# One joint tile for the q and k weights, loads in waves, more transposes by DMA and a new instruction order in an attention and MLP kernel

## Chip, core and metric

The kernel runs on one core of a Trainium2 chip. The metric is the device time of one execution in microseconds (us). Medians are quoted. Ratios are the mean time of one kernel's fast runs over that of the other's of the same rounds, with a 95% interval, so not quite the ratio of the medians. A run counts as fast within 1.5% of the fastest of its kernel.

Engines: PE is TensorE (matrix products), PEld its weight loads, DVE VectorE, ACT ScalarE, POOL GpSimd, SP SyncE, which here issues DMAs.

## The reference, cut to what matters

```python
x = A_x                                    # 2048 positions x 512, bf16
h  = x + attention(layernorm(x)) @ wo      # 32 heads of 16; 8 keys: positions s, s-2, ... s-14
h2 = h + ((relu(n @ W_gate) * (n @ W_up)) @ W_down)     # n = layernorm(h), 1376 hidden
```

## The kernel before

The 2048 positions are handled in four chunks of 512 positions (chunk 0 to 3), each of four tiles of 128 rows. Each chunk has a first norm of x, transposed so that features lie on partitions; the q, k and v products (PE); the attention, mostly large elementwise products on DVE; the output projection with the residual; a second norm of h, transposed too; and the gate, up and down products (PE).

All steps are collected in a plan, and a list of numbers, RANK, gives each step its place on its engine. So the order of every engine's queue is a part of the program, and is fixed when it runs.

Some transposes are done by DMA, issued from SP. And for chunks 0 to 2 the first additions of the attention's tree are *accumulating* DMAs, issued from POOL (`ta`), of 512 KB each:

```python
DACC = tuple((k, t) for k in range(3) for t in range(4))       # chunk, head group
TDD, TDL = 2.4, 1.6                         # planned issue and latency of a DMA transpose
DMAT = (("h",2,0),("h",2,2),("x",3,0),("x",3,2))   # h: second norm, x: first; chunk; first tile of a pair
# ... in layernorm(), for a pair of tiles in DMAT:
nc.sync.dma_start_transpose(out=dst.t[:, :, j * P:(j + 1) * P], in_=xn.t[:])
# ... else on TensorE:
nc.tensor.transpose(tp.t[:].bitcast(BF16)[:, o:o + P], xn.t[:, t * P:(t + 1) * P], identity[:])
# ... in the attention, after the value product mu{t}:
m = add(("mu%d" % t, tk), "DVE", D40, f_mu, ...)
if n == 4 and (tk, t) in DACC:
    nc.gpsimd.dma_start(mt.t[:, 0:4, :], mt.t[:, 4:8, :], accum_op=ALU.add)
```

The softmax here doesn't subtract the row's maximum and nothing guards it: scores larger than these inputs give would overflow.

Of the kernel before, what the change touches and what calls it, by code (L numbers as in the profile page):

```python
# [18 lines left out]
    1, 3, 5, 2, 0, 4, 54, 6, 7, 30, 160, 197, 186, 250, 712, 8, 11, 10, 12, 14,  # L19
    17, 23, 27, 32, 20, 26, 31, 16, 18, 21, 24, 28, 33, 37, 9, 13, 15, 19, 22, 25,  # L20
    29, 34, 35, 65, 71, 68, 70, 73, 38, 60, 66, 56, 63, 69, 51, 61, 43, 55, 40, 50,
    45, 58, 83, 145, 79, 154, 76, 162, 74, 99, 80, 86, 96, 104, 110, 75, 67, 85, 89, 90,
    171, 179, 185, 114, 136, 123, 133, 128, 94, 113, 101, 108, 118, 148, 159, 183, 189, 193, 156, 170,
    199, 203, 205, 165, 176, 201, 204, 207, 142, 152, 181, 187, 192, 211, 218, 210, 215, 214, 222, 209,
    212, 227, 234, 221, 225, 228, 232, 226, 231, 239, 241, 246, 256, 249, 257, 261, 244, 259, 251, 260,
    264, 292, 321, 277, 317, 267, 313, 324, 333, 340, 280, 305, 270, 304, 301, 308, 303, 310, 315, 295,
    325, 307, 328, 285, 323, 319, 329, 335, 327, 344, 297, 341, 331, 346, 314, 339, 349, 350, 366, 343,
    358, 338, 365, 355, 372, 392, 334, 359, 348, 362, 397, 401, 421, 691, 717, 393, 407, 694, 718, 357,
    420, 701, 721, 363, 423, 699, 720, 39, 47, 44, 48, 36, 41, 42, 46, 49, 52, 62, 78, 64,
    77, 82, 57, 81, 59, 72, 84, 144, 191, 124, 188, 91, 178, 102, 182, 88, 164, 109, 169, 143,  # L30
    172, 117, 168, 147, 252, 139, 300, 87, 299, 151, 302, 195, 174, 224, 245, 229, 208, 238, 248, 253,
    258, 268, 273, 271, 284, 293, 296, 294, 290, 275, 283, 286, 287, 289, 298, 309, 345, 352, 318, 330,
    361, 367, 326, 337, 364, 368, 306, 316, 347, 351, 373, 378, 379, 386, 376, 382, 383, 395, 385, 389,
    391, 396, 390, 394, 398, 400, 402, 403, 406, 413, 408, 415, 419, 411, 417, 412, 418, 422, 431, 456,
    427, 454, 433, 460, 426, 452, 494, 439, 469, 441, 471, 434, 462, 436, 463, 500, 438, 466, 437, 465,
    479, 488, 464, 474, 503, 487, 496, 484, 491, 489, 498, 493, 501, 507, 450, 518, 458, 517, 506, 523,
    499, 520, 526, 447, 508, 444, 509, 524, 516, 536, 709, 726, 510, 530, 707, 725, 522, 538, 705, 723,
    533, 537, 703, 722, 98, 105, 92, 97, 93, 103, 53, 95, 112, 116, 126, 132, 125, 130, 146, 131,
    137, 129, 135, 150, 167, 216, 177, 217, 184, 220, 194, 223, 161, 240, 157, 237, 163, 242, 153, 213,
    173, 428, 175, 409, 202, 416, 219, 356, 236, 254, 265, 312, 274, 263, 288, 320, 322, 332, 336, 342,  # L40
    360, 353, 377, 375, 369, 374, 371, 384, 387, 381, 380, 430, 435, 453, 459, 414, 429, 446, 449, 424,
    432, 451, 457, 399, 425, 443, 448, 467, 473, 461, 468, 475, 482, 470, 478, 477, 480, 472, 476, 485,
    486, 481, 483, 490, 495, 519, 521, 511, 513, 528, 531, 497, 502, 543, 559, 540, 558, 549, 568, 548,
    565, 573, 560, 585, 567, 582, 575, 588, 544, 561, 594, 556, 578, 583, 593, 554, 576, 579, 590, 596,
    552, 570, 563, 580, 546, 564, 553, 574, 591, 616, 625, 572, 618, 599, 621, 608, 623, 631, 620, 630,
    587, 628, 633, 626, 642, 715, 731, 612, 639, 713, 729, 597, 635, 711, 727, 600, 640, 714, 730, 100,
    106, 115, 121, 111, 119, 107, 120, 122, 127, 140, 149, 155, 166, 134, 141, 138, 158, 247, 281, 180,
    255, 196, 269, 190, 266, 243, 279, 235, 278, 200, 272, 230, 276, 233, 541, 198, 505, 262, 550, 206,
    545, 291, 282, 311, 404, 370, 354, 388, 405, 410, 440, 442, 492, 445, 504, 529, 534, 527, 532, 455,
    525, 514, 515, 512, 542, 562, 581, 586, 535, 539, 555, 569, 551, 557, 566, 571, 547, 577, 584, 589,  # L50
    595, 603, 604, 611, 598, 607, 592, 601, 606, 609, 614, 615, 610, 613, 602, 605, 617, 619, 622, 624,
    636, 637, 641, 627, 634, 629, 632, 638, 646, 660, 650, 663, 647, 661, 644, 656, 675, 667, 677, 665,
    674, 673, 681, 670, 678, 684, 659, 671, 654, 668, 657, 669, 662, 672, 682, 651, 664, 652, 666, 643,
    655, 645, 658, 679, 683, 695, 648, 686, 680, 693, 649, 689, 697, 653, 688, 676, 690, 696, 685, 706,
    728, 736, 692, 700, 716, 732, 687, 702, 719, 734, 698, 704, 724, 735, 708, 710, 733, 737,
# [36 lines left out]
class Plan:  # L92
# [21 lines left out]
    GUIDE = ()  # L114

    def order(self):
        for kx, cx, ky, cy in self.GUIDE:
            xs = [o for o in self.ops if o.key and o.key[0].startswith(kx) and o.key[1] == cx]
            for o in self.ops:
                if o.key and o.key[0].startswith(ky) and o.key[1] == cy:  # L120
                    o.deps += xs
        waiting = list(self.ops)
        free = {}
        while waiting:
            best = {}
            for op in waiting:
# [45 lines left out]
            waiting.remove(op)  # L172
# [4 lines left out]
def kernel(  # L177
# [55 lines left out]
    w3_sb = [sb.tile([P, NT, D], BF16, name=f"w{n}_sb") for n in "qkv"]  # L233
# [32 lines left out]
    def setup():  # L266
# [4 lines left out]
        for c, q in enumerate((nc.sync, nc.scalar, nc.sync)):  # L271
            q.dma_start(w3_sb[c][:], w3_r[:, :, c * D:(c + 1) * D])
        for tk in range(1, NCK):
            nc.sync.dma_start(x_sm[:, tk * BPC:(tk + 1) * BPC, :], x_rows[:, tk * BPC:(tk + 1) * BPC, :])

        nc.sync.dma_start(wo_sb[:], A_wo.rearrange("(p t) f -> p t f", t=NT))
        nc.sync.dma_start(wu_sb[:], B_W_up.rearrange("(dt p) f -> p dt f", p=P))
        nc.sync.dma_start(wg_sb[:], B_W_gate.rearrange("(dt p) f -> p dt f", p=P))
        nc.sync.dma_start(
            wd_sb[:, 0:NFF, :], B_W_down[0:NFF * P, :].rearrange("(ft p) n -> p ft n", p=P))  # L280
        if FTAIL:
            nc.sync.dma_start(wd_sb[:FTAIL, NFF, :], B_W_down[NFF * P:F, :])

# [10 lines left out]
        nc.gpsimd.memset(vT[:, :, 0:PADL], 0.0)  # L294

# [22 lines left out]
    TDD, TDL = 2.4, 1.6  # L318
    NWARM = 48
    DMAT = (("h",2,0),("h",2,2),("x",3,0),("x",3,2))  # L320
# [8 lines left out]

    LNA = ((0, 0, 0, 0), (0, 0, 0, 0))  # L330
# [5 lines left out]
    A5, A10, AX, AS = 0.52, 0.92, 0.8, 0.2  # L336
    AL = 0.14
    D2, D5, D10, D20, D40, DST, DSM = 0.34, 0.62, 0.62, 1.15, 2.2, 0.6, 0.08
    DL = 0.14

    def load(t):
        return add(None, "LD", 0.0, None, lat=t)

    xload = [[load(t) for t in (3.4, 3.5, 3.9, 3.9)]] + [[load(t)] * BPC for t in (9.7, 11.2, 12.7)]
    wload = {n: load(t) for n, t in
             (("q", 6.3), ("k", 7.0), ("v", 8.3), ("o", 14.0), ("u", 18.0), ("g", 22.0), ("d", 27.0))}

    def layernorm(tk, src, dst_slots, pr, groups, on_act, residual=None):
# [7 lines left out]
        for grp in groups:  # L356
# [3 lines left out]
            for j in grp:  # L360
# [17 lines left out]
                elif tk == 0 and j == BPC - 1:  # L378

                    xns[j], sm, sq = Buf(xn_s), Buf(sm_s), mv  # L380

                    def f_su(j=j, xn=xns[j], sm=sm):
                        nc.scalar.activation(out=xn.t[:], in_=x_sm[:, j, :], func=ACT.Copy,
                                             accum_out=sm.t[:, j:j + 1])

                    def f_nm(j=j, sm=sm):
                        V.tensor_scalar(out=mv.t[:, j, 0:1], in0=sm.t[:, j:j + 1], scalar1=1.0 / D,
                                        scalar2=None, op0=ALU.mult)

                    def f_sq(j=j, xn=xns[j]):  # L390
                        nc.scalar.activation(out=xn.t[:], in_=x_sm[:, j, :], func=ACT.Square,
                                             bias=mv.t[:, j, 0:1], scale=-1.0, accum_out=mv.t[:, j, 1:2])

                    a = add(("xsu", tk), "ACT", 0.75, f_su, [src[j]], pr, take=[xns[j], sm], lat=AL)
                    a = add(("xnm", tk), "DVE", DSM, f_nm, [a], pr, take=[mv], use=[sm], lat=DL)
                    ag.append(add(("xsq", tk), "ACT", 0.75, f_sq, [a], pr, use=[mv, xns[j]], lat=AL))
                else:
                    st = Buf(st_s)

                    def f_st(j=j, st=st):  # L400
                        V.bn_stats(out=st.t[:], in_=x_sm[:, tk * BPC + j, :])

                    def f_ag(j=j, st=st):
                        V.bn_aggr(out=mv.t[:, j, :], in_=st.t[:])

                    a = add((ln + "st" + gk, tk), "DVE", DST, f_st, [src[j]], pr, take=[st], lat=DL)
                    ag.append(add((ln + "ag" + gk, tk), "DVE", DSM, f_ag, [a], pr, take=[mv], use=[st], lat=DL))
# [433 lines left out]
```

## Time and profile before

| | before |
|---|---|
| time, first three runs | 203.86 us (203.53 to 205.39) |
| span of the profiled execution | 203.6 us |
| PE busy / DVE busy | 195.4 us (96%) / 155.1 us (76%) |
| granted TensorE clock, mean of the span | 0.983 |

PE is full from 10 us to 200 us, so the time is the moment at which PE starts, plus its work, plus the tail.

### The profile page before, as it was taken

The numbers are of one execution on the slowest core, as the hardware profiler recorded it, in microseconds if no ns is written. First come the engines' busy times: TensorE is split into PE (matmuls) and PEld (weight loads), VectorE is DVE, ScalarE is ACT, GpSimd is POOL, SyncE is SP. The second block draws the span as 40 slices with busy tenths as digits, with TensorE's granted clock in tenths as the row PEclk, the third lists the DMA queues.
The fourth block names the chain that finished last, engine by engine and source line by source line (L and its number), as shares of the span: only waits on it lengthen the run. The fifth ranks groups of instructions, "written<-read, shape, count | busy, mean of one in ns | idle before, by whom it ended". The sixth has DMA issues, their size and how long they took to land.

```text
span 203.6 us, 2957 instructions
## 1 busy us (share of the span) xinstructions
PE 195.4 (96%) x1102; PEld 96.8 (48%) x1123; DVE 155.1 (76%) x246; ACT 127.7 (63%) x253; POOL 12.6 (6%) x26
## 2 busy tenths in 40 slices
PE   8499999999999999999999999999999999999994
PEld 8347545555545334444454444444444445444452
DVE  6549999999999999999999966599996255021314
ACT  3517879986569993797756599703665353576400
POOL 3000000330000002400033000000000000000000
PEclk9859999999999999999999999999999999999999
DMA  5999901698000002980059900400011001100003
GB/s 187 350 379 403 322 19 30 123 203 163 3 0 0 0 3 52 192 168 0 3 103 180 209 31 0 90 13 0 3 41 62 0 0 53 53 0 0 0 3 103
DMA packets 14893, 18.04 MB, mean 89 GB/s; under 512 B 5056, under 2 KB 12192, under 8 KB 14880
## 3 DMA queue, kind: packets, MB, share of 16 engines
q1 hardware_dynamic: 12336, 10.78, 16.4%
q0 software_dynamic: 1728, 6.29, 16.3%
q10 hardware_dynamic: 816, 0.79, 1.1%
q8 instruction: 9, 0.15, 0.3%
q14 instruction: 4, 0.03, 0.0%
HBM read 8.42 MB, written 2.10 MB: 52 GB/s over the span
## 4 chain that ended last, share of the span: by engine, by line
PE 93%; DMA 4%; issue 1%; SPq 0%; DVE 0%
PE bank L736 38%; PE bank L511 22%; PE bank L773 19%; PE bank L698 7%; DMA wq_sb<-in_A_wqkv_dram 4%; PE bank L564 4%; PE bank L465 2%; PE bank L625 1%; PE bank L597 1%; SPq L270 0%; DVE row L784 0%
## 5 line engine op out<-in xcount | busy, mean ns | idle before, releaser
L736 PE MATMUL bank<-quad,wg_sb 128*128 128x512 bf16 (+1 forms) x171 | 42.3, 379 | 0.3
L736 PE MATMUL bank<-quad,wu_sb 128*128 128x512 bf16 (+1 forms) x173 | 42.3, 379 | 0.1
L743 ACT ACTIVATE gr<-bank 128x512 bf16<-128x512 f32 (+1 forms) x44 | 26.0, 604 | 23.7 <-PE bank L736 18.3
L773 PE MATMUL bank<-wd_sb,gT 128*128 128x512 bf16 (+3 forms) x184 | 39.7, 366 | 0.2
L558 DVE TENSOR_TENSOR big<-quad,kT 128x4096 bf16<-128x4096 bf16 x16 | 36.0, 2284 | 0.1
L646 DVE TENSOR_TENSOR big<-big,vT 128x4096 bf16<-128x4096 bf16 x16 | 35.8, 2283 | 0.3 <-ACT big L631 0.3
L740 ACT CAST up_sb<-bank 128x512 bf16<-128x512 f32 (+1 forms) x44 | 25.7, 594 | 12.3 <-PE bank L736 8.5
L756 DVE TENSOR_TENSOR gT<-gr,up_sb 128x1024 bf16<-128x1024 bf16 (+1 forms) x24 | 15.4, 643 | 20.4 <-ACT gr L743 14.1
L773 PEld LDWEIGHTS <-gT 128*128 128x128 bf16 (+1 forms) x187 | 18.0, 98 | 19.3 <-issue 0.4
L736 PEld LDWEIGHTS <-wu_sb 128*128 128x128 bf16 (+1 forms) x176 | 17.3, 100 | 20.7 <-issue 1.3
L736 PEld LDWEIGHTS <-wg_sb 128*128 128x128 bf16 (+1 forms) x176 | 17.3, 100 | 20.6 <-issue 1.1
L511 PE MATMUL bank<-quad,wq_sb 128*128 128x512 bf16 (+1 forms) x70 | 16.9, 382 | 2.5 <-DMA wq_sb<-in_A_wqkv_dram 2.1
L631 ACT CAST big<-bank 128x512 bf16<-128x512 f32 x32 | 17.2, 610 | 1.5 <-PE bank L625 1.3
L511 PE MATMUL bank<-quad,wk_sb 128*128 128x512 bf16 (+1 forms) x70 | 16.8, 373 | 0.1
L678 POOL DMA_DIRECT2D big<-big x12 | 10.7, 894 | 98.3 <-DVE big L646 95.2
L784 DVE TENSOR_TENSOR row<-x_sm,bank 128x512 bf16<-128x512 bf16 (+1 forms) x17 | 10.6, 652 | 7.8 <-PE bank L773 7.8
L649 DVE TENSOR_TENSOR big<-big 128x1024 bf16<-128x1024 bf16 (+2 forms) x24 | 16.4, 727 | 0.0
L709 DVE SCALAR_TENSOR_TENSOR x_sm<-x_sm,bank 128x512 bf16<-128x512 bf16 x16 | 10.9, 685 | 6.8 <-PE bank L698 6.7
L511 PE MATMUL bank<-quad,wv_sb 128*128 128x512 bf16 x62 | 15.4, 379 | 0.1
L698 PE MATMUL bank<-wo_sb,quad 128*128 128x512 bf16 x61 | 14.8, 379 | 0.2
L371 ACT ACTIVATE row<-x_sm,mv 128x512 bf16<-128x512 bf16 x16 | 11.5, 717 | 4.5 <-DVE mv L363 4.4
L519 ACT CAST quad<-bank 128x512 bf16<-128x512 f32 x16 | 9.6, 601 | 7.4 <-PE bank L511 7.4
(65 smaller groups left out, 161.7 us busy)
## 6 DMA issues: line engine op xcount, KB each, us to landing
big<-big POOLq DMA_DIRECT2D x12, 512.0 KB, 5.5
out_dram<-row SPq DMA_DIRECT2D x15, 128.0 KB, 1.7
x_sm<-in_A_x_dram SPq DMA_DIRECT2D x3, 512.0 KB, 11.0
wu_sb<-in_B_W_up_dram SPq DMA_DIRECT2D x1, 1376.0 KB, 10.6
wg_sb<-in_B_W_gate_dram SPq DMA_DIRECT2D x1, 1376.0 KB, 13.9
wd_sb<-in_B_W_down_dram SPq DMA_DIRECT2D x1, 1280.0 KB, 15.7
wq_sb<-in_A_wqkv_dram SPq DMA_DIRECT2D x1, 512.0 KB, 8.4
wk_sb<-in_A_wqkv_dram ACTq DMA_DIRECT2D x1, 512.0 KB, 8.6
```

The lines of the kernel that those rows point to most:

```text
L371: nc.scalar.activation(out=xn.t[:], in_=h.t[:] if h else x_sm[:, tk * BPC + j, :], func=ACT.Square, bias=mv.t[:, j, 0:1], scale=1.0, accum ...
L511: nc.tensor.matmul(mm.t[:, lo:hi], lhsT=w3_sb[c][:, dt, t:D:NT], rhs=xnT.t[:, dt, lo:hi], start=(dt == 0), stop=(dt == NT - 1))
L558: V.tensor_tensor(out=pb.t[:].rearrange("p (t w) s -> p t w s", t=2), in0=q4, in1=k4, op=ALU.mult)
L631: nc.scalar.copy(out=ab.t[:, w, :], in_=bc.t[:])
L646: V.tensor_tensor(out=mt.t[:], in0=ab.t[:], in1=v8, op=ALU.mult)
L649: V.tensor_tensor(out=mt.t[:, 0:n, :], in0=mt.t[:, 0:n, :], in1=mt.t[:, n:2 * n, :], op=ALU.add)
L698: nc.tensor.matmul(od.t[:], lhsT=OT.t[:, t, j * P:(j + 1) * P], rhs=wo_sb[:, t, :], start=(t == 0), stop=(t == NT - 1 and tk not in RPE))
L736: nc.tensor.matmul(mm.t[:fs, :], lhsT=w_sb[:, dt, ft * P: ft * P + fs], rhs=hnT.t[:, dt, :], start=(dt == 0), stop=(dt == NT - 1))
L740: nc.scalar.copy(out=ub.t[:fs, i, :], in_=um.t[:fs, :])
L743: nc.scalar.activation(out=gr.t[:fs, i, :], in_=gm.t[:fs, :], func=ACT.Relu)
L756: V.tensor_tensor(out=gt.t[:fs, 0:n, :], in0=gr.t[:fs, 0:n, :], in1=ub.t[:fs, 0:n, :], op=ALU.mult)
L773: nc.tensor.matmul(od.t[:, c0:c1], lhsT=gts[ft].t[:fs, ft % 2, j * P:(j + 1) * P], rhs=wd_sb[:fs, ft, c0:c1], start=(ft == 0), stop=(ft == ...
```

## The change

It means to start PE earlier and with a warm clock, and to take 16 transposes off it: the q and k weights go to one tile, loaded by four DMAs in pieces of 2 KB; later loads are held back by small copies on POOL until earlier ones have landed ("waves"); chunk 0's first norm is made in four groups of one tile; 8 idle products after each of the first two transpose groups keep the clock up; chunk 3's second norm is transposed by DMA. The whole order is new, made with lower planned costs for a DMA transpose. The residuals were on DVE already.

```diff
-    w3_sb = [sb.tile([P, NT, D], BF16, name=f"w{n}_sb") for n in "qkv"]
+    wqk_sb = sb.tile([P, NT, 2 * D], BF16, name="wqk_sb")
+    wv_sb = sb.tile([P, NT, D], BF16, name="wv_sb")
...
+        for dt in range(NT):
+            (nc.scalar if dt % 2 else nc.sync).dma_start(wqk_sb[:, dt:dt + 1, :], w3_r[:, dt:dt + 1, 0:2 * D])
...
+        nc.gpsimd.tensor_copy(out=x_sm[0:1, BPC, 0:1], in_=x_sm[0:1, 0, 0:1])
+        nc.sync.dma_start(x_sm[:, BPC:2 * BPC, :], x_rows[:, BPC:2 * BPC, :])
+        nc.gpsimd.tensor_copy(out=wv_sb[0:1, 0, 0:1], in_=wqk_sb[0:1, NT - 1, 0:1])
+        nc.sync.dma_start(wv_sb[:], w3_r[:, :, 2 * D:3 * D])
+        nc.gpsimd.tensor_copy(out=x_sm[0:1, 2 * BPC, 0:1], in_=x_sm[0:1, BPC, 0:1])
...
-    TDD, TDL = 2.4, 1.6
-    NWARM = 48
-    DMAT = (("h",2,0),("h",2,2),("x",3,0),("x",3,2))
+    TDD, TDL = 1.25, 1.5
+    NWARM, NFILL = 44, 8
+    DMAT = (('h',2,0),('h',2,2),('x',3,0),('x',3,2),('h',3,0),('h',3,2))
...
-        groups = [[0, 1], [2], [3]] if tk == 0 else [[0, 1, 2, 3]]
+        groups = [[0], [1], [2], [3]] if tk == 0 else [[0, 1, 2, 3]]
...  (all numbers of RANK are new, and the queues follow it strictly)
```

## The prediction

> **What bounds the kernel now.** I read the page's slices first, then the chain of waits, then the start on a finer scale.
>
> The slices (40 of 5.09 us; tenths of busy time, and the clock granted to TensorE):
>
> ```profile
> PE   8499999999999999999999999999999999999994
> DVE  6549999999999999999999966599996255021314
> PEclk9859999999999999999999999999999999999999
> ```
>
> TensorE (PE) is full from the third slice to the last; VectorE (DVE) is full only up to about 110 us. The two weak spots are the second slice, where PE is at 4 tenths, and the second and third of the clock row, 8 and 5 tenths. The chain of waits, in order of time (start us, us, what; pieces left out), with the pieces that the change touches:
>
> ```profile
> 1.66 8.42 DMA wq_sb<-in_A_wqkv_dram
> 10.08 0.05 issue
> 10.13 2.32 PE bank L511 x9
> 12.45 0.22 issue
> 12.67 7.27 PE bank L511 x38
> ...
> 166.88 0.22 PE bank L465 x4
> 167.11 1.73 PE bank L773 x8
> 168.83 0.45 PE bank L465 x8
> 169.28 0.65 PE bank L773 x3
> 169.93 0.23 PE bank L465 x4
> ...
> 194.39 6.27 PE bank L773 x39
> ```
>
> One load (8.42 us), then TensorE from 10.13 to 200.66 without a wait worth naming. So the time is start of the q and k products + TensorE work + about 3 us of tail (last addition and store). Only these terms can move: when TensorE starts, how fast its clock is then, and how many instructions stand in its queue. Finer stretches (us, PE busy, clock, DMA share, GB/s):
>
> ```profile
> 8.50:9.00 0.50, 0.00 (x0) 0.80 1.05 375
> 9.00:9.50 0.50, 0.00 (x0) 0.50 1.09 387
> ...
> 15.00:15.50 0.50, 0.50 (x3) 0.50 1.10 408
> 15.50:16.00 0.50, 0.50 (x3) 0.88 1.00 397
> ```
>
> A mean of 0.80 over 8.5 to 9.0 puts the drop to half clock at 8.8; 0.88 over 15.5 to 16.0 puts the return at 15.6. From 10.13 to 15.62 the first products therefore ran at half speed: 5.5 us for 2.75 us of work.
>
> **What the Trainium skill says.** "TensorE: Matmul & The Clock Gate", Part 1 (the HAM clock gate): the array drops to half clock after a window of about 3.4 us with too little activity and returns after a busy one, and the window runs freely, so that its phase differs from run to run. The trace agrees: 8.8 to 15.6 is 6.8 us, two such windows. Same page, Part 4 (PE-mode transpose): transposes do not count as activity as matmuls do. That fits: 16 transposes ran between 6.7 and 8.1 us and the clock fell all the same; one trace can't prove it. "DMA: Bandwidth & Descriptors", Issuing engines are not separate DMA queues: all loads run on the same 16 engines and interleave. The trace agrees: q and k, issued at 1.66 us, landed after 8.4 and 8.6 us, v after 9.6, and by my sum of the GB/s some 2.66 MB had moved by 10 us, though the first x tiles, q and k are only 1.57 MB. Same page, Why small descriptors are slow: about 3 cycles per packet beside 32 bytes per cycle. 1 KB pieces then cost 35 cycles and 2 KB ones 67, so the wider pieces save 3 cycles in 70, some 4% of 1.05 MB at 350 GB/s: 0.1 us, an estimate from that page. No run shows it yet.
>
> **The change, part by part.** The title's "residuals on DVE" and the DMA transposes of chunk 2's second norm and chunk 3's first are already in the kernel before; new among those is only chunk 3's second norm.
>
> 1. Loads in waves. At first only the x tiles of chunk 0, the joint q and k tile and the x of chunk 1 are in flight (2.1 MB at most); v waits for the last quarter of the q and k tile, chunk 2's x for chunk 1's. From the stretches of 2 us (16, 282, 336, 351 GB/s), 1.57 MB have moved by 6.9 us and 2.1 MB by 8.4 us. Taking the middle and some latency, q and k are there at 8.0 us, against 10.08.
>
> 2. But then the norm of chunk 0 is the later of the two. Before, these rows of the timeline (start, us, what) show it done at 8.7 us, with TensorE then waiting for weights until 10.13:
>
> ```profile
> 3.48 1.29 DVE L401 BATCH_NORM_STATS2 st<-x_sm 128x6 f32<-128x512 bf16 x2 [0.29 <-DMA x_sm<-in_A_x_dram]
> 7.44 1.23 ACT L479 COPY quad<-bank 128x512 bf16<-128x512 bf16 x2 [0.61 <-PE bank L465]
> 7.51 0.75 DVE L477 COPY quad<-bank 128x512 bf16<-128x512 bf16 x2
> ```
>
> The change makes four groups of one tile and moves the fourth tile's statistics from ScalarE (ACT) to DVE. Read from the new order list, DVE does four statistics (0.64 each), four aggregates (0.15), three normalisations (0.35) and a copy (0.72) before the first half of the columns is complete: 2.56 + 0.60 + 1.05 + 0.72 = 4.93 us from 3.48, so 8.4, and with some gaps for ScalarE's logarithm and exponential (0.3 and 0.2 us a pair) 8.8. So TensorE's first product goes at 8.8, not at 8.0: 1.3 us earlier than before. One transpose group (0.25 us) now falls behind that start. Gain: about 1.05 us.
>
> 3. Fills. 44 warm-up products in place of 48, and 8 after each of the first two transpose groups, about 0.45 us each, all in front of the first product where TensorE idles: no cost on the path. Their gain is the clock. In the profiled run the loss was 2.75 us. If the clock holds, all of it comes back; if it still falls at 8.8, the window that follows is now full of products and ends at 12.2, so 3.4 us at half clock, 1.7 lost, 1.05 gained. But the profiled execution took 205.38 us and the three runs 203.53, 203.86 and 205.39; as the window's phase is free, I take the median run to have lost only about 2.75 - 1.5 = 1.25 us (my guess from that spread). From this I count 0.5 to 1.2 us for the median, 0.8 in the middle, with more possible.
>
> 4. Chunk 3's second norm leaves TensorE: 0.22 + 0.45 + 0.23 = 0.90 us of the chain. In its place SyncE's queue (SP) issues four DMA transposes. The eight of the kernel before were issued in 1.2 us each and landed 2.5 us after issue. After the last output-projection product of chunk 3, the way to the normalised, transposed tile is residual 0.77, mean 0.15, square 0.91, logarithm and exponential 0.50, one normalisation 0.35, four issues 4.8 and 1.3 more until landing: 8.8 us. The new order list gives TensorE 20 gate and up products and 44 down products of chunk 2 in that time: 64 x 0.2155 = 13.8 us. So it is hidden with 5 us to spare: gain 0.90 us.
>
> 5. Everything else in the list reorders work. Before, the table of TensorE's waits has only 0.4 us after the start, so order can gain nothing there and can only lose. DVE's start on the attention products moves up too: after the last copy at about 9.8 it has chunk 1's norm (some 5 us) to do and can start near 15.2 rather than at 18.84, 3.6 us earlier, so it shouldn't become the bound of the DVE-full stretch. I deduct 0.1 us for new small waits; the retuned durations in the diff suggest that the order was searched with care.
>
> Sum for the median: 1.05 + 0.8 + 0.90 - 0.1 = 2.65, with 0.6 added for the chance that the clock holds all along where the run before lost the full 2.75: about 3.25 us, giving 203.86 - 3.25 = 200.6 us, 1.6% less.
>
> **The rivals.** (a) The weights still bind. For it: q landed 3.2 us after the moment at which 1.57 MB had moved, so bytes alone do not tell the landing. If that lag stays, q and k come at about 9.5 to 10, the start gains nothing, and with 0.9 for the transposes and some clock the result is 202.5. Against it: less is in flight behind the tile. (b) The clock stays warm in every run and was cold in most of the runs before: 1.05 + 2.75 + 0.9 = 4.7, so 199.2 and over 2%. For it: the fills and the earlier products fill the critical window; against it: transposes and waits still leave that window only about half busy (my count is about 2 us of 3.4, against 1.8 before). (c) DVE becomes the bound. It now does more at the start, and up to 110 us it has no slack; if chunk 0's attention starts only 2 us earlier while TensorE is 3.5 us ahead, TensorE waits in 20 to 67 us and 1.5 us of the gain are lost: 202. Against it is the estimate of 15.2 us above. (d) The DMA transposes arrive late because SP must first issue stores that wait for DVE; every microsecond over the 5 spare is a wait of TensorE near 170 us. I give it little.
>
> **Range and chances.** The mechanical gains of 1.05 and 0.9 are rather sure; the clock's share runs from 0 to 2.75; rivals (a) and (c) take 1 to 2. That spans 198.4 to 202.9. Faster by over 2% needs about 199.8 or less (a gain of 4 us), which is the full clock gain with no loss elsewhere: 0.37. Slower by 2% would need a broken order: 0.02.
>
> **What would show it.** Step 1: q and k land at 7.5 to 8.8 us. Step 2: TensorE's first q or k product starts at 8.6 to 9.2, released by the copy of the transposed tile (DVE), not by the DMA. Step 3: the granted clock shows no half-speed slice after 6 us, or one window only; chunk 0's 32 q and k groups take about 7 us instead of 9.65. Step 4: 80 transposes of that line on TensorE instead of 96, 12 DMA transposes, and no wait before chunk 3's first up product. Step 5: TensorE's waits after the start stay below 1 us in sum. The prediction is wrong if the start doesn't move, if new waits of over 1.5 us stand in TensorE's row between 20 and 70 us, or if the start is warm and full and the time falls below 198.4.

## More of the kernel before

The prediction shows the lines. One that it does not show turned out to matter most. It closes the view of the transposed tiles of the kernel before, and gives the least, the middle and the largest time from issue to landing of its eight DMA transposes:

```profile
DMA to landing us min/median/max: 2.4/2.5/5.4
```

The middle value is what a transpose takes alone (e2 below). The largest is over twice that. The timeline shows what ran then: the queue of SP first, then that of POOL (start us, us, engine, line, what):

```profile
33.65 5.22 SPq L454 DMA_TRANSPOSE quad<-row  x4
37.48 1.01 POOL L678 DMA_DIRECT2D big<-big  x1 [35.04 <-DVE big L646]
```

The four transposes of chunk 3 are issued from 33.65 to 38.87 us, and the first accumulating DMA starts at 37.48, when the last transpose is still to come. Only the tail of the row overlaps.

## The result

212.69 us (211.59 to 214.1, six runs) against 203.85 us: the ratio is 1.043 (1.038 to 1.048). It is slower by 4.3%, far outside the range.

The slices of the profile after, in 40 parts of 5.31 us: busy tenths of PE, granted clock, and DMA engines.

```profile
PE   7699899980699999999999999999999999999993
PEclk9999999998599999999999999999999999999999
DMA  5689951998200000397000992032010022200012
```

The start is as forecast: no dip of the clock in the first slices. But the tenth slice of PE is empty: near 50 us it does nothing, while the DMA engines are busy for 8 tenths, and in the eleventh the clock is at 5 tenths. The waits of PE, over the whole span (engine, line waited for: us in total, times, longest us):

```profile
PE bank L525 <- DMA quad<-row: 8.3, 1, 8.3
PE bank L525 <- DMA wqk_sb<-in_A_wqkv_dram: 1.2, 2, 0.8
```

The chain of waits has the same place in order of time:

```profile
44.01 11.03 DMA quad<-row
55.04 0.14 issue
55.17 8.84 PE bank L525 x32
```

`quad<-row` is a DMA transpose; L525 are the q, k and v products. PE waited 8.3 us for one transposed tile of chunk 3's first norm, a step that the change left on the DMA where it was. And 32 products took 8.84 us where at full clock they take 32 x 0.216 = 6.9 (the prediction's chain has 1.73 us for 8). Finer stretches show why (us, PE busy, clock, DMA share, GB/s; a packet counts whole where it starts, so a share can pass 1):

```profile
46.00:50.00 4.00, 0.88 (x5) 1.00 1.62 72
50.00:54.00 4.00, 0.00 (x0) 0.74 0.68 98
54.00:58.00 4.00, 2.83 (x7) 0.50 0.11 22
```

After five idle microseconds the clock fell to half (0.74 of four microseconds puts it at 51.9 us), and the products after the wait began cold. It came back at about 58.8 us (0.90 over 58 to 62 us). These 6.9 us fit two of the windows of about 3.4 us of the Trainium skill ("TensorE: Matmul & The Clock Gate", Part 1). Wait and cold products together: 8.3 + 1.9 = 10.2 us, more than the whole loss.

The timeline tells when the transposes were issued, with the accumulating DMAs beside them:

```profile
36.42 0.73 DVE L455 TENSOR_SCALAR row<-x_sm,mv,rs 128x512 bf16<-128x512 bf16 x2
37.18 10.01 SPq L473 DMA_TRANSPOSE quad<-row  x4
41.47 0.73 DVE L455 TENSOR_SCALAR row<-x_sm,mv,rs 128x512 bf16<-128x512 bf16 x2
```

```profile
34.61 1.01 POOL L692 DMA_DIRECT2D big<-big  x1 [23.42 <-DVE big L660]
36.82 0.86 POOL L692 DMA_DIRECT2D big<-big  x1 [1.20 <-DVE big L660]
39.90 0.86 POOL L692 DMA_DIRECT2D big<-big  x1 [2.21 <-DVE big L660]
41.85 0.86 POOL L692 DMA_DIRECT2D big<-big  x1 [1.09 <-DVE big L660]
```

```profile
DMA to landing us min/median/max: 2.4/2.5/12.7
```

The new order puts two of chunk 3's normalisations (L455) behind two value products (L660), and the other two behind all four. So the transposes run from 37 us on, in the middle of the four accumulating DMAs, and one of them took 12.7 us to land. The accumulating DMAs of that stretch landed after 8.1 us in the middle, against 6.2 before.

### The profile page after: what moved, and what is told of

Read it like the earlier page. It is cut to its first block, busy times and chain, and to the rows that moved or that the text cites. A ratio compares the mean times of both kernels' runs of the same rounds, so it can differ in the third digit from the quotient of the medians.

```text
span 212.3 us, 2963 instructions
## 1 busy us (share of the span) xinstructions
PE 196.1 (92%) x1119; PEld 95.9 (45%) x1119; DVE 155.4 (73%) x247; ACT 121.9 (57%) x249; POOL 12.9 (6%) x29
## 4 chain that ended last, share of the span: by engine, by line
PE 61%; DVE 23%; DMA 12%; issue 2%; ACT 0%; POOL 0%; DVEq 0%; ACTq 0%; POOLq 0%
PE bank L750 27%; PE bank L787 18%; DVE big L572 10%; DVE big L660 7%; DMA x_sm<-in_A_x_dram 7%; PE bank L712 7%; PE bank L525 6%; DMA quad<-row 5%; DVE st L420 2%; DVE row L455 1%; PE bank L578 1%; DVE gT L770 1%; DVE ex L626 1%; PE bank L484 0%; PE bank L639 0%
## 5 line engine op out<-in xcount | busy, mean ns | idle before, releaser
L754 ACT CAST up_sb<-bank 128x512 bf16<-128x512 f32 (+1 forms) x44 | 24.8, 595 | 26.4 <-PE bank L750 18.8
L525 PE MATMUL bank<-quad,wqk_sb 128*128 128x512 bf16 (+1 forms) x144 | 30.9, 364 | 9.5 <-DMA quad<-row 8.3
L660 DVE TENSOR_TENSOR big<-big,vT 128x4096 bf16<-128x4096 bf16 x16 | 36.0, 2283 | 0.1
L525 PEld LDWEIGHTS <-wqk_sb 128*128 128x128 bf16 x144 | 15.8, 115 | 22.3 <-issue 10.9
L663 DVE TENSOR_TENSOR big<-big 128x1024 bf16<-128x1024 bf16 (+2 forms) x24 | 16.9, 730 | 3.5 <-DMA big<-big 3.4
L533 ACT CAST kT<-bank 128x512 bf16<-128x512 f32 x16 | 9.3, 615 | 12.5 <-PE bank L525 12.5
L525 PE MATMUL bank<-quad,wv_sb 128*128 128x512 bf16 x64 | 16.2, 396 | 0.0
L455 DVE TENSOR_SCALAR row<-x_sm,mv,rs 128x512 bf16<-128x512 bf16 x32 | 11.5, 403 | 4.2 <-ACT rs L437 4.2
```

The source lines that it names most:

```text
L455: V.tensor_scalar(out=xn.t[:], in0=x, scalar1=mv.t[:, j, 0:1], scalar2=rs.t[:, j:j + 1], op0=ALU.add if residual else ALU.subtract, op1=AL ...
L525: nc.tensor.matmul(mm.t[:, lo:hi], lhsT=wv_sb[:, dt, t:D:NT] if c == 2 else wqk_sb[:, dt, c * D + t:(c + 1) * D:NT], rhs=xnT.t[:, dt, lo:h ...
L660: V.tensor_tensor(out=mt.t[:], in0=ab.t[:], in1=v8, op=ALU.mult)
L663: V.tensor_tensor(out=mt.t[:, 0:n, :], in0=mt.t[:, 0:n, :], in1=mt.t[:, n:2 * n, :], op=ALU.add)
L754: nc.scalar.copy(out=ub.t[:fs, i, :], in_=um.t[:fs, :])
```

## The experiments

Three theories were set against each other. C, collision: transposing and accumulating DMAs in flight together hold each other up. L, late: the transposes are quick but issued too late. S, start: the new start delays everything after it.

### e1: chunk 3's normalisations ahead of the value products

```diff
 DVE, from 31 us (step/chunk; xxn = normalise for the first norm, mu = value product)
-xxn3/2 mu3/0 mu0/0 xxn0/3 xxn2/3 mu1/0 mu2/0 xxn3/3 xxn1/3
+xxn3/2 xxn0/3 xxn2/3 xxn3/3 xxn1/3 mu3/0 mu0/0 mu1/0 mu2/0
 ACT: chunk 3's logarithm and exponential right after the eighth copy of chunk 0's weights
```

> The changed kernel with one edit of its order list: the four normalisations of chunk 3's first norm go before chunk 0's first value product on DVE, and their logarithm and exponential on ScalarE right after the eighth copy of chunk 0's weights, so that the four DMA transposes are issued at about 33 to 38 us, before the accumulating DMAs, as in the kernel before. Theory C (collision: DMA transposes and the accumulating DMAs of chunk 0, in flight together, hold each other up): transposes land after about 2.5 us, the wait of 8.3 us and the half clock after it (32 products in 8.84 us instead of 6.9) go, 212.7 - 10.2 = 202.5 us (201 to 204.5). Theory L (late: the transposes are quick, only issued too late): the same 202.5. Theory S (start: the new loads and groups of the start delay everything after them): 210 or more.

Measured: 203.49 us against 203.96; ratio 0.998 (0.996 to 1.000). In the queue of SP the transposes stand early again:

```profile
33.02 5.27 SPq L473 DMA_TRANSPOSE quad<-row  x4
```

The longest landing is 5.0 us (5.4 in the kernel before), and PE no longer waits for a transpose. One move in an order list is worth 9.2 us. S is out as the cause of the loss; C and L are not yet told apart. And the forecast gain is still missing: 0.5 us instead of 3.25.

### e2: no accumulating DMAs in chunk 0

```diff
-    DACC = tuple((k, t) for k in range(3) for t in range(4))
+    DACC = tuple((k, t) for k in range(1, 3) for t in range(4))
```

> The changed kernel with chunk 0's four accumulating DMAs taken out; DVE makes these additions itself (4 x 1.15 us), at the place where the tree of additions goes on. Chunk 3's transposes are still issued late, from 37 to 42 us and on. Theory C: with nothing to collide with they land in about 2.5 us each, TensorE's wait for them falls from 8.3 to under 2 us; time 203 to 206. Theory L: the wait stays near 8 us, 211 to 214. Theory S: 211 to 214.

Measured: 209.31 us; ratio 1.026 (1.024 to 1.029). The transposes start as late as in the changed kernel, at 36.5 us, yet the view of the tile says of all twelve:

```profile
DMA to landing us min/median/max: 2.4/2.5/2.5
```

PE had no wait for them at all: its row is full from 46 to 54 us. So the lateness alone cost nothing there, and the whole wait of 8.3 us came from the accumulating DMAs, as C says. The time missed the expected 203 to 206, because the 4.6 us of additions now on DVE gave PE a wait of 3.6 us for the attention's result, and a cold stretch after it. The mechanism was right, the total was not.

### e3: chunk 3's first norm transposed by PE

```diff
-    DMAT = (('h',2,0),('h',2,2),('x',3,0),('x',3,2),('h',3,0),('h',3,2))
+    DMAT = (('h',2,0),('h',2,2),('h',3,0),('h',3,2))
```

> The changed kernel with the first norm of chunk 3 transposed by TensorE again (the normalisations stay late; the accumulating DMAs stay). Theory C: no DMA transposes there, so no hold-up; the wait of 8.3 us becomes under 2 us, 0.9 us of transposes come back, accumulating DMAs land in about 6 us: 203 to 205. Theory L: the late normalisations still hold TensorE up, but only until about 44 us: also 203 to 205.5. Theory S: 211 or more.

Measured: 207.22 us; ratio 1.015 (1.012 to 1.019). With the other side of the collision removed, the four accumulating DMAs of that stretch landed after 5.2 us in the middle instead of 8.1 (first the changed kernel, then e3; KB each, us to landing):

```profile
big<-big POOLq DMA_DIRECT2D x4, 512.0 KB, 8.1
big<-big POOLq DMA_DIRECT2D x4, 512.0 KB, 5.2
```

The hold-up works both ways. The time is above what was expected. PE waited 1.2 us for the copies of the transposes, which e3's order puts right before the products that read them. Another 1.6 us, for an attention product at 22 us, has nothing to do with the normalisations: DVE had waited 1.6 us for chunk 2's x in that execution (0.9 in e1).

### e4: the collision put into the kernel before

```diff
-    GUIDE = ()
+    GUIDE = (("mu0", 0, "xxn", 3),)      # these normalisations wait for the second value product
```

> The kernel before with one thing of the change alone: the four normalisations of chunk 3's first norm must wait for chunk 0's second value product, so that its DMA transposes are issued at about 39 to 44 us, among the accumulating DMAs. Start, loads and everything else as before. Theory C: transposes land after 8 to 13 us instead of 2.5, TensorE gets a wait of several us near 45 to 55 us, 207 to 214 us. Theory L: transposes land after 2.5 us, by about 46 us, and cost at most 1.5 us: 203.5 to 205.5. Theory S: 203.5 to 204.5.

Measured: 212.86 us; ratio 1.042 (1.038 to 1.046), nearly the loss of the whole change. The wait of PE, and the landing of the transposes:

```profile
PE bank L511 <- DMA quad<-row: 5.3, 1, 5.3
```

```profile
DMA to landing us min/median/max: 2.4/4.0/8.3
```

The wait and the cold products after it (24 in 8.28 us, 5.2 at full clock) make up 8.4 of the 8.9 us. The four transposes landed after 5.6 to 8.3 us, less than the 8 to 13 that C had expected. L had expected 203.5 to 205.5. No new loads, groups, fills or queues are in this kernel, but the edit is not quite alone: the planner answers it by moving four product groups of chunk 2 ahead of chunk 3's on PE, which gives the transposes more time and not less. Theory C is shown from both sides: put in, it costs 4%; taken out in three ways, the wait is gone.

### e5: two more places in the order

```diff
 DVE: the first statistic of chunk 2 (waits for a load until 16.2 us)
-... xst3/2 pr1/0 pr1/0 xst1/2 ...
+... pr1/0 pr1/0 xst3/2 xst1/2 ...
 SP, at the end
-os2/3 os1/2 os1/3 os3/3 os0/3 os4/3
+os2/3 os0/3 os1/2 os1/3 os3/3 os4/3
```

> The first experiment (e1: chunk 3's normalisations ahead of the value products, 203.49 us) with two more edits of the order list: DVE's first statistic of chunk 2, which waits for a load until 16.2 us, goes behind the first two attention products, and the last chunk's tile 0 is stored as soon as it is made, not behind two others. Theory W (what remains of the lost gain is small new waits that start at DVE's wait for chunk 2's x, and a late store): DVE's first product starts at about 15.3 to 15.8 instead of 16.8 us, TensorE's waits at 21 and 24 us (0.9 and 0.4) shrink, the end comes 0.5 us sooner after the last addition: 202.2 us (201.5 to 202.9). Theory H (these waits are covered by work elsewhere, and the order list costs nothing else): 203.0 to 203.6.

Measured: 202.86 us (202.68 to 202.98); ratio 0.995 (0.993 to 0.996). DVE's first attention product in e5 started at

```profile
15.02 4.49 DVE L572 TENSOR_TENSOR big<-quad,kT 128x4096 bf16<-128x4096 bf16 x2
```

against 16.78 in e1. This is the fastest kernel of the study and beats the kernel before by 0.5% and the changed one by 4.6% (medians), though the first is within 2% and so counts as the same.

### e6: chunk 3's second norm back on PE

```diff
-('x',3,2),('h',3,0),('h',3,2))
+('x',3,2))
```

> The first experiment (e1) with chunk 3's second norm transposed by TensorE again: the one transpose step that the change moved to the DMA, undone alone. If step 4 of the prediction holds, the 16 transposes come back into TensorE's full stretch and cost 0.9 us: 204.4 (204.0 to 204.8). If moving them bought nothing (the DMA way sets a wait of its own, or TensorE has idle room there): 203.2 to 203.7.

Measured, on e1: 205.01 us; ratio to the kernel before 1.005 (1.003 to 1.008), e1's was 0.998. The one new move to the DMA is worth 1.5 us by the medians, 0.8 by the two profiled runs (204.91 and 204.1). Read the other way, e6 is the new start in its own order without this move, and it is 1.0 us slower than the kernel before.

### e7, e8, e13, e14: the new start with the old order

```diff
 e7:  start as in the change (chunk 0's norm, q and k), all other steps as the kernel before orders them; h3 on PE
 e8:  e7, h3 by DMA
 e13: e7 with chunk 2's first statistic behind two attention products
 e14: e8 with that move, and more of chunk 2's products as cover for the transposes
```

> The new start alone (joint q and k tile, loads in waves, four groups, fills) with the order of the kernel before for everything after the first q and k products (one statistic of chunk 2 moved behind the first two attention products, as its load comes later), and chunk 3's second norm on TensorE. Theory W: the start of 1.6 us earlier comes through, less a few tenths: 202.4 us (201.8 to 203.0). Theory G (the earlier start is given back, because DVE and not TensorE sets the pace from 20 to 60 us and its work moved up less): 203.4 to 204.2.

Measured: 205.23 us; ratio 1.006 (1.004 to 1.009). DVE idled 2.9 us for chunk 2's x, which one statistic wanted early and the waves bring at 16.1 us; PE waited 1.9 us in all for normalised rows.

> As the run before this one, with chunk 3's second norm transposed by the DMA, its output projection moved together so that some 12 us of chunk 2's products cover the way. If step 4 holds: 0.9 us under the run before this one, 201.5 us (200.9 to 202.1). If the transposes are not covered, or collide with the stores: the same as that run or above it. Both kernels are meant to beat the kernel before.

Measured: 204.98 us; ratio 1.005 (1.003 to 1.007). Hardly better than e7: PE waited 1.1 us for the transposed tile, so they were not covered.

> The run with the new start alone (e7, 205.23 us), with the one statistic of chunk 2 that still stood in front of chunk 1's normalisations moved behind the first two attention products; DVE had idled 2.9 us there for a load that the waves bring at 16.1 us. Theory W (the start is worth its earlier first product, and e7 lost it to this wait, which is the waves' doing together with the old order): DVE's first attention product at about 15.2 instead of 18.0 us, TensorE's waits for chunk 1's and 2's rows (1.9) go, 202.6 to 203.4 us. Theory G (the start gains nothing against a usual, warm execution of the kernel before): 203.8 to 205.

Measured: 205.48 us; ratio 1.010 (1.005 to 1.014). The wait for the load was gone, and DVE idled 3.4 us for chunk 1's logarithm and exponential instead, which the old order has behind three copies of q and k on ACT. This miss says little of the start itself: one place moved, the next one bound.

> The same with chunk 3's second norm transposed by the DMA (e8, 204.98 us), the same statistic moved, and more of chunk 2's products between chunk 3's output projection and the transposed tile (the up and gate products first, ScalarE's squares ahead of their copies), so that the wait of 1.1 us for the transposes goes. If step 4 holds here as it did in e6: 0.9 to 1.5 us under the run before this one; if both theories W and that hold, 201.3 to 202.3 us, the fastest of all. If the DMA transposes bring nothing outside the searched order: as the run before this one.

Measured: 204.08 us; ratio 1.002 (0.999 to 1.006). Covered, the transposes by DMA bring 1.4 us under e13, but the time is far from the 201.3 to 202.3 us for both theories.

### b1: the kernel before again

> The kernel before, unchanged, to get a second profile of it. Theory M (the profile that the prediction was read from caught an execution with a cold start, which is not the usual one): granted clock 0.99 to 1.00 instead of 0.983, TensorE's first q product again at about 10.1 us but chunk 0's q and k done at about 17 us instead of 19.8, span about 202 instead of 203.6, so there were no 0.8 + 0.6 us of clock to gain. Theory U (the cold start is usual): clock 0.983 to 0.985 again, q and k done at 19.5 us or later.

Measured: 204.06 us, ratio 1.002 (0.998 to 1.006). The profile was again at clock 0.983 and 205.52 us, with q and k done at about 20 us, as theory U says. But the six other executions of the same kernel had clocks of 0.989 to 1.000 and 203.73 to 204.41 us, as theory M says. Both profiled executions were the cold exception: of 20 more executions, one (205.45 us) had 0.983, the rest 0.992 to 1.000. The cold execution of b1 was 1.5 us slower than the mean of the six others.

### e9: e5 without the fills

```diff
-    NWARM, NFILL = 44, 8
+    NWARM, NFILL = 44, 0
```

> The fifth experiment (e5, 202.86 us) without the two times eight filling products between the first transposes. If the fills hold the clock (step 3 of the prediction): a half-speed stretch appears after about 8.8 us in the profile or in most runs' mean clock (0.983 to 0.992), and the time is 203.6 to 205.5. If the clock holds without them: 202.6 to 203.1, clock 1.00.

Measured: 203.83 us; ratio 0.999 (0.993 to 1.004). The profile shows half clock while q and k are made:

```profile
9.00:10.00 1.00, 0.98 (x10) 0.75 0.21 75
10.00:11.00 1.00, 1.00 (x8) 0.50 0.64 82
```

Four of six runs had a clock of 0.988 to 0.992 and took 203.77 to 204.35 us, the two at 1.000 took 202.31 and 202.52. All runs of e5 were at 0.996 to 1.000. So the fills hold the clock of this start. But the two runs at 1.000 are also faster than all of e5, by 0.2 to 0.7 us; whether the fills cost something where the clock holds anyway is not settled.

### e10: e5 without waves

```diff
-        nc.gpsimd.tensor_copy(out=x_sm[0:1, BPC, 0:1], in_=x_sm[0:1, 0, 0:1])     # and the other two
```

> The fifth experiment (e5, 202.86 us) with the loads issued at once instead of in waves (the three small copies on GpSimd that hold them back are gone; joint q and k tile, groups and fills stay). If step 1 of the prediction holds: the q and k tile lands at about 10 us instead of 8.1 to 9.0, TensorE's second quarter of products waits for it, 203.5 to 204.5 us. If the waves bring nothing, because chunk 0's norm or DVE sets the pace and chunk 2's x comes earlier without them: 202.3 to 203.1.

Measured: 202.90 us; ratio 0.997 (0.993 to 1.001). The q and k tile landed 5.6 to 6.0 us after issue (the middles of its two queues), no later than the 6.2 to 6.4 us with waves in e5. The waves bring nothing; that part of step 1 of the prediction failed.

### e12: e10 with pieces of 1 KB

```diff
-        for dt in range(NT):
-            (nc.scalar if dt % 2 else nc.sync).dma_start(wqk_sb[:, dt:dt + 1, :], w3_r[:, dt:dt + 1, 0:2 * D])
+        for c in range(2):
+            for i, q in enumerate((nc.sync, nc.scalar)):
+                q.dma_start(wqk_sb[:, 2 * i:2 * i + 2, c * D:(c + 1) * D], w3_r[:, 2 * i:2 * i + 2, c * D:(c + 1) * D])
```

> The run without waves (e10, 202.90 us, the q and k tile landed 5.6 to 6.0 us after issue, the last quarter at about 8 us), with the same tile loaded by four DMAs of 256 KB over the same two queues, but in pieces of 1 KB, as in the kernel before, instead of 2 KB. If the size of the pieces is what brings q and k early: they land 8 to 8.5 us after issue, at about 10 us as in the kernel before, the first product that needs the last of them waits until then, and the time is 203.8 to 204.8. If it is the splitting over two queues ahead of everything else and the pieces matter by about 0.1 us (the estimate of the prediction): they land at about 8 us, 202.6 to 203.4.

Measured: 203.40 us; ratio 0.999 (0.993 to 1.004). They landed after 6.6 to 6.8 us in the middle, and PE waited 1.0 us for the last. That lies between the two expectations. With the old pieces, q and k still land 1.8 us sooner than in the kernel before (8.4 and 8.6 us). The two queues cannot be the reason, as the kernel before used the same two. Among what differs are four DMAs in place of two, and that SP issues v at 3.94 us in place of 2.13; which of them counts is not shown. The pieces may give up to 1 us, but which bytes come first differs too, so their share, and the estimate of 0.1 us, is not settled.

## Why the prediction was wrong

The failing step is 5: "Before, the table of TensorE's waits has only 0.4 us after the start, so order can gain nothing there and can only lose", followed by a deduction of 0.1 us. In place of the 0.1 us stood one wait of 8.3 us near 50 us and 1.9 us of cold products. The table told that the old order cost nothing, not what it kept apart. The order list that step 4 was read from also showed chunk 3's normalisations between the value products; I read it only for the steps that the diff names, and took it on trust that the order "was searched with care". e4 shows that the late flight costs 8.9 us without the rest of the change. Rival (d), late transposes, was the right kind of event, but was looked for at SP's stores and near 170 us, and called unlikely; so was the "broken order", with a chance of 0.02.

Why the order came out so is argued, not shown: the planned cost of a transpose was lowered from 2.4 + 1.6 to 1.25 + 1.5 us. That is right for a transpose alone (1.2 us to issue, 2.5 to land) and has no term for what else the DMA engines do. The higher cost of before may have pushed the transposes to the front.

The other steps, in the order of the prediction:

- Step 1, q and k at 8.0 us: too early. In the changed kernel the last PE wait for them ended at 9.8, as rival (a) had it, in e5 at 9.0. And the waves are not what helps (e10).
- Step 2, first product at 8.8: it went at 8.53 and in e5 at 8.37, about as worked out. But in the changed kernel it was weights, not the norm, for which it waited (0.35 us, and 0.84 us before the second pair).
- Step 3, the clock: right in mechanism (e9), wrong in size. The 0.8 + 0.6 us were taken from a profile of a cold execution; b1 shows that a cold start costs 1.5 us, not 2.75, and that usual executions have little to win back.
- Step 4, 0.90 us: right in mechanism. It measured 0.8 to 1.5 (e6) and 1.4 (e14), and only 0.25 where it was not covered (e8: a wait of 1.1).
- Step 5 on DVE's start near 15.2: e5 has 15.02. In the change it was 17.07, since a statistic stood in front that waited for a load.

Without the collision the time is 203.5 us (e1), still above the range of 198.4 to 202.9; with two more places mended, 202.86 (e5). So the collision is not the whole miss: the gain of 1.05 us from the earlier start (step 2) is seen in no run. The new start loses 1.3 us in the old order (e7) and 1.0 in its own (e6), and e5 without the move of chunk 3's second norm would be at about 204.4 us (an estimate, 202.86 plus the 1.5 of e6). Rival (c), DVE as the bound, may be why. The shares of the chain that ended last, before and in e5:

```profile
PE 93%; DMA 4%; issue 1%; SPq 0%; DVE 0%
PE 64%; DVE 25%; DMA 5%; ACT 3%; issue 2%; POOL 0%; DVEq 0%; ACTq 0%
```

DVE had next to no part in the chain before and has a quarter of it in e5. No run tests this, and no profile of a warm execution of the kernel before was caught to set beside e5.

## What to carry to other kernels

When a change comes with a new order, read the order of every DMA beside every other DMA, not only of the steps that the diff names: a transfer that is "hidden anyway" is hidden only for the company it has now. A largest landing time of twice the middle one is the hint, and costs nothing to look up. And look at the clock of all runs before explaining a dip that only the profiled one shows.

## What the Trainium skill lacked or had wrong

- "DMA: Bandwidth & Descriptors", Rules for kernel authors, says "A transpose next to ordinary DMAs needs nothing". That is about correct data, and all results of the experiments were correct. No page found gives the cost in time: DMA transposes of a 128x512 bf16 tile landed after 2.5 us alone and up to 12.7 us beside accumulating DMAs of 512 KB, whose middle landing rose from 5.2 us (e3, no transposes there) to 8.1.
- "TensorE: Matmul & The Clock Gate", Part 1, says that the cold start varies from run to run. It lacks that a profiled execution can be the exception: 0.983 in both profiles of the kernel before, 0.989 to 1.000 in the six other executions of b1, and 0.983 in one of 20 more.
